# A tile's additions directly behind its last projection, token forms one place on, and weight rounds moved away from two places

## The chip, the cores and the metric

The kernel runs on one NeuronCore of one Trainium2 chip. Time is device microseconds (us) of that core for one execution; a version is compared by the median of its runs. The engines are TensorE (PE; PEld is its weight load), VectorE (DVE), ScalarE (ACT), GpSimd (POOL) and SyncE (SP, which issues most DMA transfers). Each engine runs its own instructions in program order and waits for the others by semaphores.

## The reference

Linear attention with decay over 2 x 8 sequences of 768 tokens (head size 64, blocks of 64 tokens), then two feed-forward layers over the 1536 tokens of width 512, all in float32:

```
out[block] = ((q @ k.T) * decay) @ v + (q * lam_pow) @ kv_state      # attention, block by block
kv_state   = lam_block * kv_state + (k * rev_pow).T @ v
h = x @ w_in                                                         # layer 1: 512 -> 2048
x = where(h >= 1, h, where(h <= -1, 0, (h + 1)**2 / 4)) @ w_out      #          2048 -> 512
gate = sigmoid(x @ w_gate); val = x @ w_val                          # layer 2: 512 -> 1536
out  = (gate * val) @ w_out                                          #          1536 -> 512
```

## The kernel before

**Numbers.** Weights arrive as pairs of 32-bit words of a wider float. Each float32 operand of a matmul is split into a high part (`...h`, rounded by a ScalarE copy) and the rest (`...l`, a VectorE subtraction), and a product is three matmuls: high by high, rest by high, high by rest (L211 to L213, L265, L397). A matmul of 128x128 by 128x512 is the unit of work.

**Weight pieces.** The weights are 68 pieces of 128x512. A *weight round* (`w_round`, `w_steps`) works on three pieces at once: it copies the words of piece k from the loaded `raw` tile (ScalarE, L102 and L103: tiles `wr` and `wc`), makes the float of piece k-1 (VectorE, L109, L110, L112) and splits piece k-2 into its high part (ScalarE, L116) and its rest (VectorE, L120) in a tile `w`. It also issues the next load (SP, L95). For some pieces GpSimd forms sums of weights (L135), which are split into the tiles `s` (ScalarE L142, GpSimd L143). In the attention, `w_round_in_two` does a round in two halves, with its additions on GpSimd.

**Attention.** Sixteen units (tile numbers in `s`, `uu`, `x`). In the loop over units, iteration i puts on the queues the scores and state updates of unit i+1, the evacuation of unit i-1, the states `sc`, the first half of a weight round for the i in `ROUNDS` (5 is the first), then `blocks(i + 1)`, which copies the states into the matmul operand `st` (ScalarE, L739), then the second half and the outputs of unit i (L749 and L758). Outputs of unit i need the blocks of unit i.

**Layer 1.** 16 slices of the hidden width in five groups (4, 3, 3, 3, 3) by three token tiles t of 512. For each (slice, tile), in the order of `seq`, TensorE computes the hidden block `h` (12 matmuls), ScalarE and VectorE make the activation `r` (L241, L242, L246), and `parts` splits it into `gh` and `gl` (L233, L234). The projection of the block two places back follows `h` on TensorE (12 matmuls, L265, into four accumulators `a`). When a group's last slice of a token tile is projected, `flush` adds the four accumulators to `part[t]` (VectorE, L287; in the first group copies, two on ScalarE at L283 and two on VectorE at L285). The accumulators and the `h` blocks share the eight banks of PSUM in a ring, so a bank's next user waits until its last reader is done.

Before the change, `finish` only projects and notes the tile in `closing`; `close` does the `flush` later, after the next hidden block and the next `split` have been put on the queues. After each projection, `go_on` takes the next entry of the list `later`, if there is one, and then does a weight round unless the entry returned True:

```
def go_on():
    if not (later and later.pop(0)()):
        w_round()
```

`flush` fills `later` at the last group: `x_split` splits the finished sums into the operands `xh` and `xl` of layer 2 (L297, L298), and `x_forms` (after t = 1) adds four entries for the *token forms*: sums and differences of token tiles 0 and 1 (`sub`, L375) and their splits (L379, L380) into `xt`.

**Layer 2.** 12 slices in pairs. The first pair is computed directly (`single`): hidden blocks of the gate and the value, sigmoid (L466), product (L467), projection. The other pairs use block products (`pair`, L397): seven blocks of 6 matmuls over token tiles 0 and 1, made from token forms and weight forms, which replace eight; ScalarE copies intermediate sums out of the first bank `p0` at L417, L423 and L428, and TensorE goes on adding to the same bank. Token tile 2 is computed by `single`. Layer 2 opens two new pools of four banks each, on the memory of the old eight.

Of the kernel before, what the change touches and what calls it, by code (L numbers as in the profile page):

```python
# [30 lines left out]
ROUNDS = (5, 6, 8, 10, 11, 12, 13, 14, 15)  # L31
# [8 lines left out]
def fused_kernel(ctx: ExitStack, tc: tile.TileContext, qkv, qd, cst, w1, w2, out):  # L40
# [232 lines left out]
    later = []  # L273

    def flush(n, t, js=range(4)):
        two = n >= NF1
        begin = n == (NF1 + GF if two else GROUPS[0]) - 1
        end = n == (NF1 + NF2 if two else NF1) - 1
        for j in js:
            o = part[t][:, j]  # L280
            if begin:
                if j % 2 == 0:
                    act.activation(o, accs[j], AF.Copy)  # L283
                else:
                    dve.tensor_copy(out=o, in_=accs[j])  # L285
            else:
                dve.tensor_tensor(out=o, in0=o, in1=accs[j], op=ALU.add)  # L287
            if end and two:
                r0 = t * TT + j * P
                sp.dma_start(out=out[r0:r0 + P, :], in_=o)  # L290
        if end and not two:
            tt = slice(t * TT, (t + 1) * TT)

            def x_split(js):
                for j in js:
                    o = part[t][:, j]
                    act.activation(xh[:, j, tt], o, AF.Copy)  # L297
                    dve.tensor_tensor(out=xl[:, j, tt], in0=o, in1=xh[:, j, tt].bitcast(F32),  # L298
                                      op=ALU.subtract)


            if t < NTT - 1:
                later.extend([lambda: x_split((0, 1)), lambda: x_split((2, 3))])
            else:
                later[2:2] = [lambda: x_split(range(4))]
            if t == 1:
                x_forms()

    behind, fresh, closing = [], [], []

    def close():
        if closing:
            flush(*closing.pop())

    def go_on():

# [7 lines left out]

    def feed_forward():
        def finish():  # L330
            p = behind.pop(0)
            project(*p, now=False)
            if p[4]:
                closing.append(p[:2])
            go_on()

        for u in seq:
            n, t, first, last = u
            h = hidden(n, t, 0)
            split()  # L340
            close()
            yield
            r = act1(h, n, t)
            act1_end(r, h)
            fresh.append((u, r))
            yield
            while attention_over and len(behind) >= 2:
                finish()
        split()
        while behind:  # L350
            close()
            finish()
        close()

# [9 lines left out]
    def x_forms():  # L366
# [7 lines left out]
        def sub(o, a, b_):  # L374
            dve.tensor_tensor(out=o, in0=a, in1=b_, op=ALU.subtract)  # L375

        def split(i):
            hi, lo = dst[i]
            act.activation(hi, f[i], AF.Copy)  # L379
            dve.tensor_tensor(out=lo, in0=f[i], in1=hi.bitcast(F32), op=ALU.subtract)  # L380
# [1 line left out]


        later.extend([
            lambda: sub(x1, y1, x1) or sub(y1, y2, y1),
            lambda: sub(y2, y2, x1) or sub(x2, x2, y2) or True,
            lambda: split(0) or split(2) or True,
            lambda: split(1) or split(3),
        ])

    def product(o, w, c, x, start):
# [136 lines left out]
    with ExitStack() as actx:  # L528
# [248 lines left out]
        with tc.manual_schedule():  # L777
# [13 lines left out]
            for i in range(nu):  # L791
# [13 lines left out]
                else:  # L805
                    split()
                r = w_round_in_two() if i in ROUNDS else iter((0, 0))
                next(r)
                if i + 1 < nu:
                    blocks(i + 1)  # L810
                next(r)
                if i in HIDDEN:
                    next(steps)
                outputs(i)
# [88 lines left out]
```

## Time and profile before

| | |
|---|---|
| runs before | 616.96, 619.74 and 618.11 us; median 618.11 us |
| profiled execution | 618.94 us, with a span of 616.1 us from first to last instruction |
| TensorE busy | 597.6 us (97%) |
| VectorE busy | 431.5 us (70%) |
| ScalarE busy | 323.5 us (53%) |
| GpSimd busy | 111.2 us (18%) |
| mean granted TensorE clock | 0.992 |
| chain that ended last | TensorE 88%, VectorE 4%, DMA 4%, ScalarE 2% |

The table is read from the top: one engine is busy nearly all the time, so the question for any change is where that engine stands still. A busy share is a mean over the whole span; the views by stretch and by wait tell where the idle time lies. A granted clock of 1.00 is the upper level (2.4 GHz), 0.50 the lower (1.2 GHz). In the timeline a row of several instructions shows their common time, and the times of one engine's rows overlap a little.

### The profile page before, as it was taken

The numbers are of one execution on the slowest core, as the hardware profiler recorded it, in microseconds if no ns is written. First come the engines' busy times: TensorE is split into PE (matmuls) and PEld (weight loads), VectorE is DVE, ScalarE is ACT, GpSimd is POOL, SyncE is SP. The second block draws the span as 40 slices with busy tenths as digits, with TensorE's granted clock in tenths as the row PEclk, the third lists the DMA queues.
The fourth block names the chain that finished last, engine by engine and source line by source line (L and its number), as shares of the span: only waits on it lengthen the run. The fifth ranks groups of instructions, "written<-read, shape, count | busy, mean of one in ns | idle before, by whom it ended". The sixth has DMA issues, their size and how long they took to land.

```text
span 616.1 us, 7965 instructions
## 1 busy us (share of the span) xinstructions
PE 597.6 (97%) x3016; PEld 488.2 (79%) x3016; DVE 431.5 (70%) x701; ACT 323.5 (53%) x585; POOL 111.2 (18%) x116
## 2 busy tenths in 40 slices
PE   7999999999999999999958999999999999999997
PEld 4787888888888888888847887888888888878886
DVE  7688853777576577477693789698598598595444
ACT  6798654675565465466462467554454454441220
POOL 4379500000000000000000132341151051050000
PEclk9999999999999999999987999999999999999999
DMA  9993410223132023033020123223023033000013
GB/s 293 399 321 129 145 61 2 89 89 96 35 103 69 23 80 104 0 103 102 2 79 23 35 68 104 66 72 103 16 86 103 8 96 104 0 1 0 1 69 136
DMA packets 15813, 52.58 MB, mean 85 GB/s; under 512 B 1688, under 2 KB 2976, under 8 KB 15776
## 3 DMA queue, kind: packets, MB, share of 16 engines
q1 hardware_dynamic: 15760, 52.08, 26.3%
q8 instruction: 23, 0.38, 0.2%
q14 instruction: 14, 0.11, 0.1%
q10 hardware_dynamic: 16, 0.01, 0.0%
HBM read 48.92 MB, written 3.15 MB: 85 GB/s over the span
## 4 chain that ended last, share of the span: by engine, by line
PE 88%; DVE 4%; DMA 4%; ACT 2%; issue 1%; DVEq 0%; ACTq 0%; SPq 0%
PE a L265 35%; PE p L397 15%; PE h L211 12%; PE h L212 11%; PE h L213 11%; DMA raw<-in_w 2%; PE x L758 1%; PE s L676 1%; PE x L749 1%; DMA qp<-pd 1%; DVE part L287 1%; DMA pd<-pw 1%; DVE wr L110 1%; DVE w L120 1%; PE uu L691 1%
## 5 line engine op out<-in xcount | busy, mean ns | idle before, releaser
L211 PE MATMUL h<-xh,w 128*128 128x512 f32 x320 | 126.3, 395 | 8.3 <-DVE part L287 8.3
L212 PE MATMUL h<-xh,w 128*128 128x512 f32 x320 | 125.6, 393 | 0.0
L213 PE MATMUL h<-xl,w 128*128 128x512 f32 x320 | 125.4, 392 | 0.0
L265 PE MATMUL a<-gh,w 128*128 128x512 f32 x384 | 118.6, 390 | 0.0
L265 PE MATMUL a<-w,gh 128*128 128x512 f32 x288 | 89.0, 390 | 0.1
L265 PEld LDWEIGHTS a<-gh,w 128*128 128x128 f32 x384 | 72.1, 188 | 15.1 <-POOL w L120 0.2
L246 DVE SCALAR_TENSOR_TENSOR r<-r,h 128x512 f32<-128x512 f32 x48 | 32.9, 686 | 70.7 <-ACT r L242 70.7
L241 ACT ACTIVATE r<-h,half 128x512 f32<-128x512 f32 x48 | 33.1, 689 | 88.3 <-PE h L213 88.3
L211 PEld LDWEIGHTS h<-xh,w 128*128 128x128 f32 x320 | 60.7, 190 | 21.7 <-DVE part L287 8.7
L135 POOL TENSOR_TENSOR wr<-wr 128x256 f32<-128x256 f32 x20 | 16.1, 806 | 339.8 <-DVE w L120 339.0
L287 DVE TENSOR_TENSOR part<-part,a 128x512 f32<-128x512 f32 x108 | 68.2, 680 | 12.3 <-PE a L265 12.3
L265 PE MATMUL a<-gl,w 128*128 128x512 f32 x192 | 74.9, 390 | 0.5 <-DVE gl L234 0.5
L212 PEld LDWEIGHTS h<-xh,w 128*128 128x128 f32 x320 | 60.7, 190 | 12.6
L213 PEld LDWEIGHTS h<-xl,w 128*128 128x128 f32 x320 | 60.6, 189 | 12.6
L265 PEld LDWEIGHTS a<-w,gh 128*128 128x128 f32 x288 | 54.1, 188 | 12.0 <-DVE part L287 0.6
L265 PE MATMUL a<-w,gl 128*128 128x512 f32 x144 | 56.7, 394 | 0.0
L234 DVE TENSOR_TENSOR gl<-r,gh 128x512 fp32r<-128x512 f32 x64 | 46.0, 719 | 11.9 <-ACT gh L233 11.9
L120 DVE TENSOR_TENSOR w<-wr,w 128x512 fp32r<-128x512 f32 x61 | 51.6, 846 | 1.8 <-ACT w L116 1.8
L116 ACT ACTIVATE w<-wr 128x512 fp32r<-128x512 f32 x68 | 42.3, 622 | 19.1 <-DVE wr L112 16.1
L233 ACT ACTIVATE gh<-r 128x512 fp32r<-128x512 f32 x64 | 40.0, 625 | 22.4 <-DVE r L246 13.0
L110 DVE SCALAR_TENSOR_TENSOR wr<-raw,wr 128x512 uint32<-128x512 uint32 x68 | 50.1, 737 | 2.3
L102 ACT ACTIVATE wr<-raw 128x512 f32<-128x512 f32 x68 | 45.0, 662 | 4.5 <-DMA raw<-in_w 2.1
(92 smaller groups left out, 876.3 us busy)
## 6 DMA issues: line engine op xcount, KB each, us to landing
raw<-in_w SPq DMA_DIRECT2D x68, 512.0 KB, 3.5
u<-in_qkv SPq DMA_DIRECT2D x12, 768.0 KB, 8.1
u<-in_qkv SPq DMA_DIRECT2D x8, 384.0 KB, 6.6
out<-part SPq DMA_DIRECT2D x12, 256.0 KB, 2.0
DT<-pd SPq DMA_DIRECT2D x1, 256.0 KB, 6.2
qp<-pd SPq DMA_DIRECT2D x2, 96.0 KB, 5.5
DT<-pd SPq DMA_DIRECT2D x1, 128.0 KB
cs<-in_cst SPq DMA_DIRECT2D x1, 98.0 KB, 2.0
```

What stands on the lines that cost most here:

```text
L102: act.activation(r, hi.bitcast(F32), AF.Copy, scale=2.0 ** -112)
L110: dve.scalar_tensor_tensor(out=ru, in0=hi, scalar=0x80000000, in1=ru, op0=ALU.bitwise_and, op1=ALU.bitwise_or)
L116: act.activation(ws[i][:, 0], tmps[i][1], AF.Copy)
L120: eng.tensor_tensor(out=ws[i][:, 1], in0=r, in1=ws[i][:, 0].bitcast(F32), op=ALU.subtract)
L211: pe.matmul(h, lhsT=wh, rhs=xh[:, k, tt], start=(k == 0), stop=False)
L212: pe.matmul(h, lhsT=wl, rhs=xh[:, k, tt], start=False, stop=False)
L213: pe.matmul(h, lhsT=wh, rhs=xl[:, k, tt], start=False, stop=(k == NP - 1))
L233: act.activation(gh, g, AF.Copy)
L234: dve.tensor_tensor(out=gl, in0=g, in1=gh.bitcast(F32), op=ALU.subtract)
L265: pe.matmul(accs[j], lhsT=a, rhs=b_, start=(first and m == 0), stop=(last and m == 2))
L287: dve.tensor_tensor(out=o, in0=o, in1=accs[j], op=ALU.add)
L397: pe.matmul(o, lhsT=a, rhs=b_, start=(start and k == 0 and m == 0), stop=(k == HK - 1 and m == 2), skip_group_check=True)
```

## The change

It changes only the order in which VectorE and ScalarE get their instructions; the lists of TensorE, GpSimd and SyncE and the number of instructions are as before. Four things move. `finish` projects and flushes in one step, so a tile's additions stand directly behind the `r` of the block before (and ahead of the weight round and the split that followed). The entries of `later` start one place later (`lambda: None` does nothing, and so a round follows). The first two subtractions of the token forms return True, so no round stands beside them, the first two splits get one, and two entries at the end give the place ahead of the block products no round. In attention unit 5, `blocks(6)` comes ahead of the first half of the weight round.

```
             if t < NTT - 1:
-                later.extend([lambda: x_split((0, 1)), lambda: x_split((2, 3))])
+                later.extend([lambda: None, lambda: x_split((0, 1)), lambda: x_split((2, 3))])
             else:
-                later[2:2] = [lambda: x_split(range(4))]
+                later[3:3] = [lambda: x_split(range(4))]
...
-    behind, fresh, closing = [], [], []
-
-    def close():
-        if closing:
-            flush(*closing.pop())
+    behind, fresh = [], []
...
         def finish():
-            p = behind.pop(0)
-            project(*p, now=False)
-            if p[4]:
-                closing.append(p[:2])
+            project(*behind.pop(0))
             go_on()
...
             split()
-            close()
             yield
...
         later.extend([
-            lambda: sub(x1, y1, x1) or sub(y1, y2, y1),
+            lambda: sub(x1, y1, x1) or sub(y1, y2, y1) or True,
             lambda: sub(y2, y2, x1) or sub(x2, x2, y2) or True,
-            lambda: split(0) or split(2) or True,
+            lambda: split(0) or split(2),
             lambda: split(1) or split(3),
+            lambda: None, lambda: True,
         ])
...
                 r = w_round_in_two() if i in ROUNDS else iter((0, 0))
-                next(r)
+
+                if i != ROUNDS[0]:
+                    next(r)
                 if i + 1 < nu:
                     blocks(i + 1)
-                next(r)
+                for _ in r:
+                    pass
```

What it does to three places follows; line numbers are those of each version, and the number behind a tile's name is its allocation. First VectorE at the step from layer 1 to layer 2, before: the end of a weight round (L120), the first two subtractions of the token forms (`part_79` is `part[0]`, `part_1004` is `part[1]`), a round, the additions of token tile 2 (`part_1005`), and the first product of layer 2.

```order
L120 TENSOR_TENSOR w_2993<-wr_2791,w_2993 128x512
L375 TENSOR_TENSOR part_79<-part_1004,part_79 128x1024
L375 TENSOR_TENSOR part_1004<-part_1004 128x1024
L109 TENSOR_SCALAR wr_2995<-wr_2995 128x512
L110 SCALAR_TENSOR_TENSOR wr_2995<-raw_2796,wr_2995 128x512
L112 ISA wr_2995<-wr_2995,wc_2996 128x1024
L120 TENSOR_TENSOR w_3019<-wr_2963,w_3019 128x512
L287 TENSOR_TENSOR part_1005<-part_1005,a_2_0_2938 128x512
L287 TENSOR_TENSOR part_1005<-part_1005,a_2_1_2942 128x512
L287 TENSOR_TENSOR part_1005<-part_1005,a_2_2_2946 128x512
L287 TENSOR_TENSOR part_1005<-part_1005,a_2_3_2950 128x512
L467 TENSOR_TENSOR r_0_3065<-r_0_3065,h_0_512_3052 128x512
```

The same place in the changed kernel.

```order
L120 TENSOR_TENSOR w_2993<-wr_2795,w_2993 128x512
L287 TENSOR_TENSOR part_1005<-part_1005,a_2_0_2938 128x512
L287 TENSOR_TENSOR part_1005<-part_1005,a_2_1_2942 128x512
L287 TENSOR_TENSOR part_1005<-part_1005,a_2_2_2946 128x512
L287 TENSOR_TENSOR part_1005<-part_1005,a_2_3_2950 128x512
L364 TENSOR_TENSOR part_79<-part_1004,part_79 128x1024
L364 TENSOR_TENSOR part_1004<-part_1004 128x1024
L457 TENSOR_TENSOR r_0_3053<-r_0_3053,h_0_512_3040 128x512
```

The four additions moved up to stand directly behind L120, the two subtractions (now L364) behind them, and the round away, behind later token forms.

Second ScalarE ahead of the first pair of block products, before: the last copy of `part[1]`, a weight round with two form copies (L142), the last `gh` of layer 2's first pair, the copy out of the first bank (L417), a round, and the next two copies and a sigmoid.

```order
L283 ACTIVATE part_1004<-a_1_2_3292 128x512
L116 ACTIVATE w_3368<-wr_3238 128x512
L102 ACTIVATE wr_3370<-raw_3243 128x512
L103 ACTIVATE wc_3371<-raw_3243 128x512
L142 ACTIVATE s_0_3377<-wr_3169 128x512
L142 ACTIVATE s_1_3380<-wr_3021 128x512
L233 ACTIVATE gh_2_3383<-r_2_3342 128x512
L417 ACTIVATE q_0_3390<-p_0_3387 128x512
L116 ACTIVATE w_3403<-wr_3305 128x512
L102 ACTIVATE wr_3405<-raw_3314 128x512
L103 ACTIVATE wc_3406<-raw_3314 128x512
L423 ACTIVATE q_1_3391<-p_0_3387 128x512
```

In the changed kernel (L407 and L413 are the copies of L417 and L423):

```order
L283 ACTIVATE part_1004<-a_1_2_3292 128x512
L233 ACTIVATE gh_2_3365<-r_2_3342 128x512
L407 ACTIVATE q_0_3372<-p_0_3369 128x512
L116 ACTIVATE w_3385<-wr_3238 128x512
L102 ACTIVATE wr_3387<-raw_3243 128x512
L103 ACTIVATE wc_3388<-raw_3243 128x512
L142 ACTIVATE s_0_3394<-wr_3169 128x512
L142 ACTIVATE s_1_3397<-wr_3100 128x512
L413 ACTIVATE q_1_3373<-p_0_3369 128x512
```

The round with the form copies moved from ahead of `gh` and the first copy to behind them, and so ahead of the second copy.

Third ScalarE in attention units 5 and 6, before: the scaled keys `kd`, the two word copies of the first weight piece, the blocks of unit 6, the evacuation `xh` of unit 5.

```order
L652 ACTIVATE kd_427<-u_177,DT 128x3x64 x2
L102 ACTIVATE wr_437<-raw_181 128x512
L103 ACTIVATE wc_438<-raw_181 128x512
L739 ACTIVATE st_99<-sc_97 64x3x64 x2
L769 ACTIVATE xh<-x_443 128x384
```

And in the changed kernel.

```order
L642 ACTIVATE kd_427<-u_177,DT 128x3x64 x2
L729 ACTIVATE st_99<-sc_97 64x3x64 x2
L102 ACTIVATE wr_439<-raw_181 128x512
L103 ACTIVATE wc_440<-raw_181 128x512
L759 ACTIVATE xh<-x_443 128x384
```

The blocks moved ahead of the two word copies.

## Rows read from the trace of the kernel before

**Rows 1.** The page: the span, and TensorE's busy time, share and instructions.

```profile
span 616.1 us, 7965 instructions
...
PE 597.6 (97%) x3016; PEld 488.2 (79%) x3016; DVE 431.5 (70%) x701; ACT 323.5 (53%) x585; POOL 111.2 (18%) x116
```

**Rows 2.** Waits of TensorE: us in total, times, longest.

```profile
PE h L211 <- DVE part L287: 8.3, 1, 8.3
PE x L758 <- ACT st L739: 1.5, 2, 1.1
...
PE p L397 <- ACT q L417: 1.0, 1, 1.0
```

**Rows 3.** Busy us (instructions) by stretch: PE, PEld, DVE, ACT, POOL; granted clock; DMA.

```profile
20.00:30.00 10.00, 8.94 (x124) 7.54 (x125) 6.75 (x19) 7.42 (x19) 3.00 (x3) 1.00 1.02 417
370.00:400.00 30.00, 29.03 (x127) 23.48 (x126) 23.91 (x36) 19.87 (x36) 8.15 (x8) 1.00 0.29 81
400.00:450.00 50.00, 50.00 (x220) 40.83 (x219) 39.74 (x59) 23.30 (x42) 14.22 (x13) 1.00 0.23 68
```

**Rows 4.** Timeline of TensorE around the layer step: start, us, instruction, [idle before].

```profile
316.56 0.39 PE L265 MATMUL a<-gl,w 128*128 128x512 f32 x1
325.26 0.80 PE L211 MATMUL h<-xh,w 128*128 128x512 f32 x1 [8.31 <-DVE part L287]
...
330.01 0.39 PE L213 MATMUL h<-xl,w 128*128 128x512 f32 x1
```

**Rows 5.** Timeline of VectorE at the same place.

```profile
317.25 0.68 DVE L120 TENSOR_TENSOR w<-wr,w 128x512 fp32r<-128x512 f32 x1
317.85 1.22 DVE L375 TENSOR_TENSOR part<-part,part 128x1024 f32<-128x1024 f32 x1
...
322.74 2.47 DVE L287 TENSOR_TENSOR part<-part,a 128x512 f32<-128x512 f32 x4
```

**Rows 6.** Half microseconds of that stop; granted clock behind the POOL column.

```profile
319.00:319.50 0.50, 0.00 (x0) 0.00 (x0) 0.47 (x2) 0.48 (x2) 0.00 (x0) 1.00 0.82 336
319.50:320.00 0.50, 0.00 (x0) 0.00 (x0) 0.50 (x1) 0.50 (x1) 0.00 (x0) 0.59 0.09 33
```

**Rows 7.** Chain that ended last, layer 1 and ahead of the first pair.

```profile
297.15 2.72 PE a L265 x12
...
371.09 0.62 ACT w L116
...
372.83 0.98 ACT s L142 x2
...
374.28 0.60 ACT q L417
```

**Rows 8.** Timeline of TensorE at the first pair of blocks.

```profile
371.08 0.62 PE L397 MATMUL p<-xh,w 128*128 128x512 f32 x2
...
374.92 0.73 PE L397 MATMUL p<-xth,s 128*128 128x512 f32 x2 [0.97 <-ACT q L417]
```

**Rows 9.** Timeline of ScalarE at attention units 5 and 6.

```profile
27.13 0.70 ACT L102 ACTIVATE wr<-raw 128x512 f32<-128x512 f32 x1 [2.08 <-DMA raw<-in_w]
...
28.29 0.72 ACT L739 ACTIVATE st<-sc 64x192 f32<-64x192 f32 x2
...
31.40 0.61 ACT L739 ACTIVATE st<-sc 64x128 f32<-64x128 f32 x2
```

**Rows 10.** Timeline of TensorE there: the state part of unit 6.

```profile
29.15 0.68 PE L758 MATMUL x<-qs,st 128*128 128x128 f32 x4 [1.06 <-ACT st L739]
```

**Rows 11.** Timeline of VectorE there: the states that the block copy reads.

```profile
25.31 0.59 DVE L717 SCALAR_TENSOR_TENSOR sc<-sc,qp,uu 128x64 f32<-128x64 f32 x2
```

**Rows 12.** Timeline of VectorE at a tile's end in layer 1.

```profile
287.69 0.69 DVE L246 SCALAR_TENSOR_TENSOR r<-r,h 128x512 f32<-128x512 f32 x1 [1.76 <-ACT r L242]
...
290.69 0.68 DVE L234 TENSOR_TENSOR gl<-r,gh 128x512 fp32r<-128x512 f32 x1
291.29 2.47 DVE L287 TENSOR_TENSOR part<-part,a 128x512 f32<-128x512 f32 x4
```

More of the change, by code (lines that the diff above doesn't have):

```diff
@@ L350, in feed_forward @@
         while behind:
-            close()
             finish()
-        close()
     HK = NP // 2
```

## The prediction

> **What bounds the kernel now.** I read the engine totals first, then who waits for whom, then the busy time by stretches, and the timeline only where those point. TensorE is busy 597.6 of 616.1 us [rows 1], so 18.5 us are all that any reordering can give back, and only where TensorE stands still. Its matmuls, weights and projections are not touched: the change moves additions, copies and weight rounds on VectorE and ScalarE alone, and TensorE issues the same list as before. So the question is which of TensorE's stops ends earlier. Three of its waits lie where the change moves something [rows 2]: one of 8.3 us for an addition at L287, 1.5 us for a copy at L739 (two waits, the longest 1.1 us) and one of 1.0 us for a copy at L417. By stretches, TensorE is idle 1.06 us between 20 and 30 us and 0.97 us between 370 and 400 us, and not at all between 400 and 450 us [rows 3]. Where it does not stop, a shorter queue on VectorE is worth nothing.
>
> The 8.3 us stop is the step between the layers. TensorE's last projection of layer 1 ends at 316.56 + 0.39 = 316.95 us and the next matmul starts at 325.26 us [rows 4]. It goes into the bank of the last accumulator of token tile 2, and that bank comes free when VectorE has added the accumulator to `part`. VectorE starts these four additions only at 322.74 us and ends them at 325.21 us, 0.05 us before TensorE goes on [rows 5]. Before them it runs two large subtractions (the token forms) and one weight round, from 317.85 us on.
>
> **Part 1: the additions ahead of the token forms, and no round at the sums.** In the new order the four additions follow VectorE's L120 directly, and the two subtractions come behind; the round that stood there moves behind the next sums. The last projection is over at 316.95 us, so the additions can start where the first subtraction started, at 317.85 us. With the 2.47 us that they took [rows 5] they end at 320.32 us, and TensorE goes on at 320.37 us in place of 325.26 us: **4.89 us** gained. Everything ahead of 317.85 us on VectorE keeps its order in this place, so I see no reason for a later start. What is late next: the two subtractions now lie behind the additions until 322.8 us, and the round behind the next token forms (a subtraction takes 1.22 us, so the round takes 4.89 less two of these, 2.45 us [rows 5]). Their cover is TensorE's own work. Twelve matmuls take 2.72 us at full clock [rows 7]; the first projection of layer 2 stands behind six such blocks, the first block that reads token tile 2 behind ten (eight blocks and two projections). That is 336.7 and 347.6 us at the earliest. VectorE has its last operand of that projection after the block that ends at 331.3 us and two operations of some 0.7 us, and can split token tile 2 (four operations, 2.5 us like the additions) right after the block that ends at 336.7 us, by about 341 us. So the two margins are some 4 and 6.6 us, more than a round. If that cover were gone, a round ahead of a needed operand would cost up to its 2.45 us.
>
> **Part 2: the clock behind the stop.** The granted clock is 1.00 until 319.5 us and 0.59 in the next half microsecond [rows 6]: about 2.6 us into the stop it fell from the upper level (2.4 GHz) to the lower (1.2 GHz), and it came back after TensorE had worked again. From 325.26 to 330.01 us TensorE started 11 matmuls [rows 4]; at full clock they take 11/12 of 2.72 us, 2.49 us [rows 7], so the low clock cost 4.75 - 2.49 = 2.26 us. The new stop lasts 320.37 - 316.95 = 3.42 us. That is more than the 2.6 us after which the clock fell here, and more than the 1.06 us stop at 29 us with which it stayed at 1.00 [rows 3]. The bounds are 0 (it falls again and stays low as long) and 2.26 us (it does not fall). Neither end has a row near it: I take **1.0 us**, on the view that it falls in more than half of the executions, and that the shorter stop then leaves a shorter slow stretch.
>
> The Trainium skill, page "TensorE: Matmul & The Clock Gate", section "HAM oscillation — how this bites in real kernels", says that an idle gap between bursts of matmuls sends the engine back to half rate, so that the next burst starts cold. The trace agrees for the stop of 8.3 us; for one of 3.4 us no row here shows it. By that rule this part would give nothing and the sum would be 6.5 us.
>
> **Part 3: no round ahead of the first pair of blocks.** TensorE's second block in the pair's first bank waits 0.97 us for ScalarE's copy at L417 [rows 8], which ran at 374.28 us [rows 7]. In the old order ScalarE did a weight round with two form copies and one more copy ahead of it. In the new order the round stands behind it, and only `gh` is left in front. The first bank's six matmuls start at 371.08 us and take half of 2.72 us, so they end at some 372.5 us; the copy then runs until 373.2 us, and TensorE is occupied by the second bank's block until 373.8 us. So the wait goes. What is late next is the copy at L423, which now stands behind that round: `w`, two word copies and two form copies, which took from 371.09 to 373.81 us in the old place, 2.7 us [rows 7]. It ends at about 373.2 + 2.7 + 0.6 = 376.5 us, and TensorE wants it after two more blocks, at 373.8 + 2.72 = 376.5 us. There is no margin, so I count **0.9 us** and not 0.97; the bounds are 0 (the new wait is as long as the old) and 0.97 us. The other rounds of layer 2 move by one place in the first two pairs and by none after that, in stretches where TensorE has no wait now [rows 3].
>
> **Part 4: attention unit 5.** ScalarE stands 2.08 us for the first weight load, copies its words at 27.13 us, and only then, at 28.29 us, writes the state blocks of unit 6 [rows 9]; TensorE waits 1.06 us for them, until 29.15 us [rows 10]. In the new order the block copy stands ahead of the words. Its last input is written by VectorE from 25.31 to 25.90 us [rows 11], so its 0.72 us fit wholly into the wait for the load, and TensorE loses nothing there: 1.06 us. A part is given back at once. ScalarE's run from the load on is shorter by the block copy alone, 0.72 us, and the blocks of unit 7, which TensorE needs next, end at 31.40 + 0.61 us today [rows 9]. So from there the gain is **0.72 us**. TensorE does not stop again until layer 1, and so it is carried on. Bounds: 0 (if the second load lands late) and 1.06 us.
>
> **Part 5: the other fourteen token tiles of layer 1.** Here the additions (for the first group of slices two copies on VectorE and two on ScalarE) go ahead of `gl`, and in some tiles ahead of a round too. For one such tile: VectorE ends L246 at 288.38 us, `gl` runs at 290.69 us, the additions at 291.29 us for 2.47 us [rows 12]. In the new order the additions run to 290.9 us, the round of 2.3 us to 293.2 us and `gl` to 293.9 us. The projection that reads this `gl` starts at 297.15 us [rows 7]. The margin is 3.2 us; the next L246 starts behind the same sum of work. So this costs nothing and, since TensorE has no wait there, gives nothing. If the cover were gone it would cost up to 2.47 us a tile.
>
> **Sum.** 4.89 + 1.0 + 0.9 + 0.72 = 7.5 us. The profiled execution took 618.94 us with a span of 616.1 us; it would take 611.4 us with a span of 608.6 us. The median of the runs, 618.11 us, is 0.8 us under the profiled time, so the forecast is 618.11 - 7.5 = **610.6 us**.
>
> **The rivals.**
> A. *Layer 2 takes it back.* TensorE arrives some 7 us earlier in work whose operands VectorE makes, and then waits for a round, a token form or the copy at L423. Against it: the margins of 4 and 6.6 us above, and no waits from 400 to 450 us. For it: VectorE is busy 23.9 of 30 us between 370 and 400 us [rows 3], and the copy at L423 has no margin. If parts 2 and 3 are lost and one round stands in the way, 4.89 + 0.72 - 2.45 = 3.2 us remain: 614.9 us.
> B. *The clock does not fall at all*: 1.26 us more than I count, 609.3 us. For it: the stop is less than half as long as the old one. Against it: 3.42 us is longer than the 2.6 us at which it fell.
> C. *The bank is not what holds TensorE.* If the first block of layer 2 needed something else that ends at about the same time, the stop would stay: gain 0.9 + 0.72, 616.5 us. Against it: the 0.05 us between the last addition and the first matmul.
> D. *Slower: `gl` is late in layer 1.* The place is the projection two blocks behind a tile's end; it decides once `gl` is more than 3.2 us later than now, where the sum above says 2.5 us. If each of fourteen tiles lost 1 us, the gain of 7.5 us would turn into a loss of 6.5 us: 624.6 us; from 0.54 us a tile there is no gain left.
>
> **How the numbers follow.** The forecast with the clock falling has 0.58, B 0.30, A 0.06, C 0.03, D 0.03. The likely cases lie between the sum of the lower bounds, 4.9 us (613.2 us), and that of the upper, 4.89 + 2.26 + 0.97 + 1.06 = 9.2 us (608.9 us). With half a microsecond for the runs, which lie up to 1.6 us from their median, the range is 608.4 to 613.7 us; A, C and D are left out. No change within 0.5% means 615.0 to 621.2 us, about what these runs can tell from nothing. Forecast, B and half of A are faster: 0.91; C and the rest of A the same: 0.06; D slower: 0.03.
>
> **What would show it.** Part 1: the wait of TensorE's L211 for L287 falls to about 3.4 us, with the four additions directly behind L120. Part 2: the granted clock of the 20 us from that stop on, and the spacing of the first 11 matmuls, 0.43 or 0.23 us. Part 3: no wait for L417, and at most 0.2 us for L423. Part 4: no TensorE wait at 28 us, and layer 1 starts 0.7 us earlier. Part 5: no new waits of projections for `gl`. The prediction is wrong if the stop stays over 5 us, or if TensorE's busy share falls behind 345 us.

## The result

The changed kernel takes 609.96 us, the median of 4 runs (608.39 to 612.54), beside 618.23 us (616.96 to 619.74) for the kernel before: the ratio is 0.9867, with a 95% interval of 0.9841 to 0.9893, 8.3 us faster. The profiled execution took 610.30 us with a span of 608.4 us. The forecast was 610.6 us.

The page of the changed kernel, as in [rows 1]: the span and TensorE's totals.

```profile
span 608.4 us, 7945 instructions
...
PE 596.9 (98%) x3016; PEld 487.4 (80%) x3016; DVE 429.4 (71%) x701; ACT 323.1 (53%) x585; POOL 110.9 (18%) x116
```

TensorE's work is the same (596.9 against 597.6 us of busy time) and its idle time fell from 18.5 to 11.5 us. The waits of TensorE in the changed kernel (us in total, times, longest), which answer to [rows 2]:

```profile
PE h L211 <- DVE part L287: 2.2, 1, 2.2
...
PE a L265 <- DVE gl L234: 0.5, 1, 0.5
PE a L265 <- DVE gl L433: 0.4, 1, 0.4
PE x L748 <- ACT st L729: 0.4, 1, 0.4
```

The wait for the additions went from 8.3 to 2.2 us, the waits for the state blocks from 1.5 to 0.4, and the one for ScalarE's copy out of the first bank (1.0) is gone. What is left of the waits for the state blocks lies at 11.56 us; the kernel before has the same one, 0.4 us at 11.73. One wait is new: 0.4 us for `gl` at L433. The wait for `gl` at L234 stands in the kernel before too, at 0.5 us.

By stretches, as in [rows 3] and [rows 6] (busy us and instructions of PE, PEld, DVE, ACT and POOL, granted clock, DMA):

```profile
20.00:30.00 10.00, 9.82 (x136) 8.24 (x134) 6.98 (x19) 7.67 (x20) 3.00 (x3) 1.00 1.02 417
318.00:318.50 0.50, 0.00 (x0) 0.00 (x0) 0.50 (x2) 0.00 (x0) 0.00 (x0) 1.00 0.93 360
318.50:319.00 0.50, 0.20 (x1) 0.20 (x2) 0.50 (x2) 0.00 (x0) 0.00 (x0) 0.56 0.86 352
321.50:322.00 0.50, 0.50 (x3) 0.37 (x2) 0.50 (x1) 0.00 (x0) 0.00 (x0) 0.53 0.00 0
322.00:322.50 0.50, 0.50 (x4) 0.41 (x3) 0.34 (x1) 0.00 (x0) 0.00 (x0) 1.00 0.00 0
370.00:400.00 30.00, 29.55 (x130) 23.86 (x129) 21.36 (x32) 16.59 (x30) 7.47 (x7) 1.00 0.22 71
```

The clock still falls in the stop between the layers, in the half microsecond from 318.5 on, and is back at 1.00 from 322.0 on. Between 370 and 400 us TensorE is busy 29.55 us in place of 29.03. The timeline of TensorE, for [rows 4], [rows 8] and [rows 10]:

```profile
28.19 0.71 PE L748 MATMUL x<-qs,st 128*128 128x128 f32 x4
...
31.09 1.29 PE L748 MATMUL x<-qs,st 128*128 128x128 f32 x6
...
316.18 0.39 PE L265 MATMUL a<-gl,w 128*128 128x512 f32 x1
318.80 0.79 PE L211 MATMUL h<-xh,w 128*128 128x512 f32 x1 [2.24 <-DVE part L287]
...
321.96 0.42 PE L212 MATMUL h<-xh,w 128*128 128x512 f32 x1
322.21 0.39 PE L213 MATMUL h<-xl,w 128*128 128x512 f32 x1
...
366.43 0.40 PE L387 MATMUL p<-xl,w 128*128 128x512 f32 x1
366.67 0.62 PE L387 MATMUL p<-xth,s 128*128 128x512 f32 x2
...
398.03 0.50 PE L265 MATMUL a<-w,gl 128*128 128x512 f32 x1 [0.45 <-DVE gl L433]
```

The last projection of layer 1 ends at 316.18 + 0.39 = 316.57 us and TensorE goes on at 318.80: a stop of 2.24 us, where 3.42 had been forecast. The matmuls from 318.80 to 321.96 stand some 0.43 us apart, those behind 322.21 some 0.23. At 366.67 the block that waited 0.97 us in [rows 8] follows at once. VectorE at the layer step, for [rows 5], and in the last two rows at the projection that waits for `gl`:

```profile
316.87 0.68 DVE L120 TENSOR_TENSOR w<-wr,w 128x512 fp32r<-128x512 f32 x1
317.47 2.48 DVE L287 TENSOR_TENSOR part<-part,a 128x512 f32<-128x512 f32 x4
319.86 1.22 DVE L364 TENSOR_TENSOR part<-part,part 128x1024 f32<-128x1024 f32 x1
321.12 1.22 DVE L364 TENSOR_TENSOR part<-part 128x1024 f32<-128x1024 f32 x1
...
394.83 0.67 DVE L425 TENSOR_TENSOR q<-q,p 128x512 f32<-128x512 f32 x1
396.14 1.84 DVE L433 TENSOR_TENSOR gl<-q,gh 128x512 fp32r<-128x512 f32 x1 [0.63 <-ACT gh L435]
```

The four additions stand directly behind L120, as the change says, and run from 317.47 to 319.95 us. But TensorE starts at 318.80, after two of them, and the chain that ended last says the same:

```profile
317.55 1.21 DVE part L287 x2
```

ScalarE, for [rows 9], at the first pair of blocks, and ahead of the late `gl`:

```profile
26.11 0.73 ACT L729 ACTIVATE st<-sc 64x192 f32<-64x192 f32 x2 [0.78 <-DVE sc L707]
27.56 0.69 ACT L102 ACTIVATE wr<-raw 128x512 f32<-128x512 f32 x1 [0.72 <-DMA raw<-in_w]
...
365.50 0.60 ACT L407 ACTIVATE q<-p 128x512 f32<-128x512 f32 x1 [0.92 <-PE p L387]
...
392.65 0.64 ACT L142 ACTIVATE s<-wr 128x512 fp32r<-128x512 f32 x1 [0.94 <-POOL wr L135]
394.95 0.64 ACT L142 ACTIVATE s<-wr 128x512 fp32r<-128x512 f32 x1 [1.66 <-POOL wr L135]
395.49 0.61 ACT L435 ACTIVATE gh<-q 128x512 fp32r<-128x512 f32 x1
```

### The profile page after: what moved, and what is told of

Read it like the earlier page. It is cut to its first block, busy times and chain, and to the rows that moved or that the text cites. A ratio compares the mean times of both kernels' runs of the same rounds, so it can differ in the third digit from the quotient of the medians.

```text
span 608.4 us, 7945 instructions
## 1 busy us (share of the span) xinstructions
PE 596.9 (98%) x3016; PEld 487.4 (80%) x3016; DVE 429.4 (71%) x701; ACT 323.1 (53%) x585; POOL 110.9 (18%) x116
## 4 chain that ended last, share of the span: by engine, by line
PE 87%; DVE 5%; DMA 4%; ACT 1%; issue 1%; POOL 1%; SPq 0%; DVEq 0%; ACTq 0%; POOLq 0%
PE a L265 35%; PE p L387 15%; PE h L211 11%; PE h L212 11%; PE h L213 11%; DMA u<-in_qkv 2%; DMA raw<-in_w 2%; PE x L748 1%; PE s L666 1%; PE x L739 1%; DVE wr L110 1%; DVE w L120 1%; DVE part L287 1%; DVE gl L433 1%; POOL wr L135 1%
## 5 line engine op out<-in xcount | busy, mean ns | idle before, releaser
L110 DVE SCALAR_TENSOR_TENSOR wr<-raw,wr 128x512 uint32<-128x512 uint32 x68 | 51.5, 758 | 2.3
L233 ACT ACTIVATE gh<-r 128x512 fp32r<-128x512 f32 x64 | 40.0, 625 | 20.9 <-DVE r L246 11.5
L120 DVE TENSOR_TENSOR w<-wr,w 128x512 fp32r<-128x512 f32 x61 | 48.9, 801 | 1.8 <-ACT w L116 1.8
L234 DVE TENSOR_TENSOR gl<-r,gh 128x512 fp32r<-128x512 f32 x64 | 44.6, 696 | 7.7 <-ACT gh L233 7.7
L112 DVE CUSTOM_DVE_ANT_0 wr<-wr,wc 128x1024 uint16<-128x1024 uint16 x60 | 45.2, 753 | 2.7
```

The costliest lines, as they stand in the source:

```text
L110: dve.scalar_tensor_tensor(out=ru, in0=hi, scalar=0x80000000, in1=ru, op0=ALU.bitwise_and, op1=ALU.bitwise_or)
L112: eng.tensor_tensor(out=ri, in0=ri, in1=c, op=ALU.add)
L120: eng.tensor_tensor(out=ws[i][:, 1], in0=r, in1=ws[i][:, 0].bitcast(F32), op=ALU.subtract)
L233: act.activation(gh, g, AF.Copy)
L234: dve.tensor_tensor(out=gl, in0=g, in1=gh.bitcast(F32), op=ALU.subtract)
```

## The experiments

Each ratio is to the kernel before in the same rounds: 618.70 us (617.11 to 620.51) for the first four runs below (step_only, other_tiles, sums_first, free_bank), 618.26 (617.33 to 620.51) for free_again and gh_first, 618.72 (617.06 to 619.61) for the others. To compare parts I use points of the traces: when TensorE's last projection of layer 1 ends, when its first matmul of layer 2 starts, and so on. A trace is of one execution.

**step_only: the layer step alone.** The kernel before, with only the last tile's additions moved directly behind its last projection.

```
-                later[2:2] = [lambda: x_split(range(4))]
+                later[3:3] = [lambda: x_split(range(4))]
...
-            if p[4]:
+            if p[:2] == (NF1 - 1, NTT - 1):
+                flush(*p[:2])
+            elif p[4]:
                 closing.append(p[:2])
```

> The kernel before with one edit: the four additions of the last token tile stand directly behind its last projection, ahead of the two subtractions and the round; all other tiles, the rounds and the attention as before. In this kernel the first block of layer 2 is given the bank of the fourth accumulator, as in the kernel before. Theory (the step between the layers holds most of the gain, and TensorE goes on after the addition that frees its bank): the stop falls from 8.3 to 3.4 us, that is by 4.9 us, and the low clock behind it costs 1 to 2.3 us as before; time 612 to 613.5 us. Rival one (TensorE always goes on after the second addition when they stand behind L120): the stop is 2.2 us. Rival two (the gain lies in the rounds left out or in the other tiles): 618 us.

It took 612.51 us (611.58 to 612.87), ratio 0.9902 (0.9882 to 0.9922). VectorE's additions in its timeline:

```profile
318.49 2.48 DVE L287 TENSOR_TENSOR part<-part,a 128x512 f32<-128x512 f32 x4
```

And TensorE around the stop:

```profile
317.21 0.39 PE L265 MATMUL a<-gl,w 128*128 128x512 f32 x1
321.02 0.50 PE L211 MATMUL h<-xh,w 128*128 128x512 f32 x1 [3.42 <-DVE part L287]
```

The additions end at 318.49 + 2.48 = 320.97 us and TensorE goes on 0.05 us later, after the fourth. The stop is 3.42 us, to the hundredth what part 1 of the prediction gives. So part 1 was right for this edit alone, and the other 1.2 us of the changed kernel come from another edit.

**other_tiles: all tiles but the last.** The kernel before, with the additions of all other tiles moved and those of the last left where they were.

```
-                later.extend([lambda: x_split((0, 1)), lambda: x_split((2, 3))])
+                later.extend([lambda: None, lambda: x_split((0, 1)), lambda: x_split((2, 3))])
...
-            if p[4]:
+            if p[4] and p[:2] != (NF1 - 1, NTT - 1):
+                flush(*p[:2])
+            elif p[4]:
                 closing.append(p[:2])
```

> The kernel before with the additions of all other token tiles of layer 1 directly behind their last projection, and the last tile's additions late as before. In this kernel the first block of layer 2 is given the bank of the second accumulator, since banks are given in the order in which they come free. Theory (moved additions cost nothing in layer 1, and which of the four additions frees the bank is set by the tiles before): no new waits of projections for gl, and the stop ends after the second addition, 7.1 us instead of 8.3; time 1.2 us less, 617.0 us. Rival (gl is late in layer 1): waits of L265 for L234 in 14 tiles, above 620 us. Rival (which addition frees the bank is set by the last tile's own order): stop 8.3 us, 618.2 us.

It took 617.26 us (616.57 to 617.90), ratio 0.9977 (0.9965 to 0.9990). VectorE's additions at the layer step:

```profile
323.08 2.47 DVE L287 TENSOR_TENSOR part<-part,a 128x512 f32<-128x512 f32 x4
```

TensorE there:

```profile
316.91 0.39 PE L265 MATMUL a<-gl,w 128*128 128x512 f32 x1
324.41 0.79 PE L211 MATMUL h<-xh,w 128*128 128x512 f32 x1 [7.12 <-DVE part L287]
```

The additions still come late, behind both subtractions and a round, but TensorE goes on at 324.41 us, after the second: 323.08 plus two of 0.62 is 324.3. The stop is 7.12 us in place of 8.31. In layer 1 nothing got slower: the one wait of its projections for `gl` at L234 is 0.5 us as before, and from the first hidden block to the end of the last projection it takes 277.58 us, beside 277.55 before and 277.57 in the changed kernel.

The allocation in the programs says why. The pool that opens with layer 2 hands out its banks in the order 4, 7, 6, 5, so the first hidden block gets bank 4 in all four kernels. Which accumulator of layer 1's last tile lies in bank 4 depends on the ring before it, in which nearly every tile gets the bank that came free first in the order of the program, and so on the place of every release:

| kernel | banks of the last tile's accumulators 1 to 4 | who held bank 4 | stop, us |
|---|---|---|---|
| before | 3, 2, 0, 4 | fourth | 8.31 |
| step_only | 3, 2, 0, 4 | fourth | 3.42 |
| other_tiles | 6, 4, 0, 2 | second | 7.12 |
| changed | 6, 4, 0, 2 | second | 2.24 |

Moving the other tiles' additions moved the accumulators of the last tile to other banks. An addition takes 0.6 us, so two of them are 1.2 us.

**sums_first: the two subtractions ahead of the additions.** The changed kernel, still without a round there, but with the old order of subtractions and additions at the last tile.

```
-            project(*behind.pop(0))
+            p = behind.pop(0)
+            end = p[:2] == (NF1 - 1, NTT - 1)
+            project(*p, now=not end)
             go_on()
+            if end:
+                flush(*p[:2])
```

> The changed kernel with the two subtractions of the token forms ahead of the last tile's additions again, still without a round beside them. Theory (each VectorE operation ahead of the additions is paid in full): the stop is 2.2 + 2.45 = 4.7 us against 2.2 us in the changed kernel, time 612.4 us or, with a longer slow stretch, up to 613.4 us. Rival (leaving out the round at the sums is what matters, the place of the additions is not): 610.0 us.

It took 613.76 us (613.11 to 614.21), ratio 0.9920 (0.9902 to 0.9937). VectorE at the layer step:

```profile
317.62 1.22 DVE L368 TENSOR_TENSOR part<-part,part 128x1024 f32<-128x1024 f32 x1
318.87 1.23 DVE L368 TENSOR_TENSOR part<-part 128x1024 f32<-128x1024 f32 x1
320.02 2.47 DVE L287 TENSOR_TENSOR part<-part,a 128x512 f32<-128x512 f32 x4
```

TensorE there:

```profile
321.35 0.80 PE L211 MATMUL h<-xh,w 128*128 128x512 f32 x1 [4.58 <-DVE part L287]
```

The stop is 4.58 us, 2.34 more than in the changed kernel: the two subtractions of 1.22 us. The time is a little above the 612.4 to 613.4 us expected: the slow stretch behind the stop is longer too, with 18.79 us for the first six blocks of layer 2 against 17.94 in the changed kernel. The round is the difference to other_tiles, which has the same bank and a round between the subtractions and the additions: 7.12 - 4.58 = 2.54 us (2.45 in part 1). So the old stop of 8.31 us is made up of 2.24 that remain, 2.34 for the subtractions, 2.54 for the round and 1.19 for the bank.

**free_bank and free_again: a bank with no reader.** The changed kernel, with one tile opened and let go ahead of layer 2, so that the first block gets bank 7, where no accumulator of the last tile lies. VectorE writes one element of that tile, and nothing reads it.

```
     def second_layer():
+        dve.memset(bank("skip")[:, 0:1], 0.0)
```

> The changed kernel with one more VectorE write of one element into a spare tile of the new pool, so that the first block of layer 2 is given a bank that came free long ago, and the second block the bank of the first accumulator. Theory (what is left of the stop, 2.2 us, is the wait for that bank alone, and the clock fell because of it, 1.6 us): no stop for L287, granted clock 1.00 throughout, 3.0 to 3.8 us less than the changed kernel, 606.5 us. Rival (the operands of layer 2, made by VectorE and ScalarE, are the next bound): a wait of similar length for gl or xl a few blocks later, 609 to 610 us.

> The changed kernel with a free bank for the second layer's first block, once more, as the partner of the run before in the same rounds and for the clock: no stop between the layers, the clock at 1.00 through the layer step, about 606.9 us, 0.45 us more than its partner if the queue on ScalarE sets the wait for gl. Rival: without a stop the clock can fall all the same, and single executions lie 1.5 to 2.3 us above.

They took 606.95 us (605.64 to 607.95), ratio 0.9809 (0.9788 to 0.9831), and 606.41 us (605.68 to 607.00), ratio 0.9809 (0.9796 to 0.9822): faster than the kernel before and the changed kernel. TensorE at the layer step of the first:

```profile
316.53 0.39 PE L265 MATMUL a<-gl,w 128*128 128x512 f32 x1
316.76 0.39 PE L211 MATMUL h<-xh,w 128*128 128x512 f32 x1
```

VectorE's additions there:

```profile
317.83 2.47 DVE L287 TENSOR_TENSOR part<-part,a 128x512 f32<-128x512 f32 x4
```

TensorE goes from the projection into layer 2 with no stop, over a microsecond before the first addition begins. So at this place only the bank held it; none of its operands did. From the first matmul of layer 2 to the first projection, which stands behind the sixth block, it takes 16.32 us here and 17.94 in the changed kernel, so the restart and the low clock had cost 1.62 us. With a restart at full clock, in step_only, the six blocks take 16.47 us; so 0.15 of it is the restart. The clock is 1.00 through this stretch in the profiled executions of free_bank, free_again and step_only.

**blocks_first: the attention edit alone.** The kernel before, with only this:

```
-                next(r)
+                if i != ROUNDS[0]:
+                    next(r)
                 if i + 1 < nu:
                     blocks(i + 1)
-                next(r)
+                for _ in r:
+                    pass
```

> The kernel before with only the attention units' edit: the five block copies of the state stand ahead of the weight words on ScalarE. Theory: TensorE's wait for the state (1.06 us at 29.15) goes to nothing or to the 0.4 us that the changed kernel keeps in the next unit, the rest of the kernel stays: 0.57 to 0.72 us faster than before, ratio about 0.999, the waits for the additions (8.3) and for ScalarE's sum (0.97) unchanged. Rival: the weights' words, now later, make a weight late in the first layer and the gain is lost: no faster than before, and a wait for w or wr in TensorE's list that was not there.

It took 618.08 us (616.88 to 619.09), ratio 0.9990 (0.9980 to 1.0000), which alone would not tell it from nothing. The trace does: the waits for L739 have left the list of TensorE's waits, and from the state updates of unit 6 to the first hidden block TensorE takes 39.95 - 25.19 = 14.76 us, against 39.40 - 24.09 = 15.31 before and 39.00 - 24.26 = 14.74 in the changed kernel. That is 0.55 to 0.57 us less. But the same stretch takes 14.63 us in other_tiles, which has no edit in the attention, so its length alone does not show what the edit is worth. What else moves it is the landing of the first weight load. Times from the start of unit 6's state updates:

| kernel | edit in the attention | ScalarE's first word copy, us | TensorE's state part of unit 9, us | difference |
|---|---|---|---|---|
| before | no | 3.04 | 13.19 | 10.15 |
| other_tiles | no | 2.11 | 12.26 | 10.15 |
| changed | yes | 3.30 | 12.63 | 9.33 |
| free_again | yes | 3.02 | 12.28 | 9.26 |

In all twelve traces the difference is 10.15 to 10.17 us without the edit and 9.26 to 9.35 with it. So at an equal landing of the load the edit is worth 0.8 to 0.9 us.

**round_kept: the round ahead of the block products put back.** The changed kernel without the last line of the list of entries.

```
-            lambda: None, lambda: True,
```

> The changed kernel with the weight round ahead of the block products of the first pair put back where it was. Theory: the wait of TensorE for ScalarE's sum (0.97 us before the change) returns, the new wait for VectorE's low part gl on ScalarE's side of the pair (0.45 us in the changed kernel) goes, so that the whole is 0.5 us slower than the changed kernel, about 610.5 us beside 610.0 in the same rounds. Rival 1: the new wait does not come from the round left out: both waits stand, 0.97 us slower, about 611. Rival 2: neither wait sets anything, since later waits take the time up: the same to 0.1 us. The stop between the layers stays at 2.2 us in all three.

It took 609.71 us (609.65 to 611.80), beside 609.41 us (608.40 to 611.07) for the changed kernel in the same rounds: the medians don't separate them; 0.5 us had been expected. TensorE's wait for ScalarE in the list of waits:

```profile
PE p L386 <- ACT q L406: 1.0, 1, 1.0
```

TensorE's timeline at the pair of blocks and at the projection with `gl`:

```profile
368.65 0.72 PE L386 MATMUL p<-xth,s 128*128 128x512 f32 x2 [0.98 <-ACT q L406]
...
399.08 0.61 PE L265 MATMUL a<-w,gh 128*128 128x512 f32 x2
399.60 0.50 PE L265 MATMUL a<-w,gl 128*128 128x512 f32 x1
```

The wait of 0.98 us is back and the one for `gl` is gone: at 399.60 its matmul follows 0.52 us behind the row before, which holds two. From the pair's first matmul to the third block TensorE takes 3.86 us (3.84 before, 2.73 in the changed kernel); the projection with `gl` takes 2.92 us (2.93 before, 3.46 in the changed kernel); the pair's third and fourth blocks take 2.87 us (2.86 before, 2.75 in the changed kernel). Against the kernel before, leaving the round out gains 1.11 + 0.11 and costs 0.53: **0.69 us** net. The other traces bear it out: from the pair's first matmul to TensorE's last, the six with the round take 240.86 to 240.99 us, and the five without it and without gh_first's edit 240.18 to 240.33.

**gh_first: why `gl` is late.** On top of free_bank, ScalarE's `gh` of the second pair's first block ahead of the two copies `s` that wait for GpSimd.

```
-            w_round()
+            split = [n for n in forms if n not in ready]
+            w_steps()
             rb, gb = next(b), {}
-            ha = single(n0, 2, pair_act(n1, rb, gb))
+            xb = pair_act(n1, rb, gb)
+            next(xb)
+            for n in split:
+                w_forms_split(n)
+            ha = single(n0, 2, xb)
```

> The kernel with a free bank for the second layer's first block, and in each pair of the second layer ScalarE's rounding gh of the second pair's first block put ahead of the two copies s that wait for GpSimd's weight forms. Theory of the 0.45 us wait of TensorE for gl: it is the queue on ScalarE (the copies s wait 0.94 and 1.66 us for GpSimd, gh stands behind them), so with gh ahead of them gl comes about 0.5 us earlier, the wait goes, and the kernel takes 0.45 us less than its partner in the same rounds, with nothing slow later. Rival: gl is late by VectorE's own 1.84 us (0.69 elsewhere) beside GpSimd's work, and the wait stays at about 0.4 us wherever gh stands. Second rival: the copies s, now later, make TensorE wait for s in the next pair, and the time is the same or more.

ScalarE at that place:

```profile
392.33 0.63 ACT L435 ACTIVATE gh<-q 128x512 fp32r<-128x512 f32 x1 [3.22 <-DVE q L423]
392.87 1.14 ACT L142 ACTIVATE s<-wr 128x512 fp32r<-128x512 f32 x2
```

VectorE's `gl`:

```profile
393.00 0.69 DVE L433 TENSOR_TENSOR gl<-q,gh 128x512 fp32r<-128x512 f32 x1
```

TensorE's projection that reads it:

```profile
394.35 0.62 PE L265 MATMUL a<-w,gh 128*128 128x512 f32 x2
394.81 0.39 PE L265 MATMUL a<-w,gl 128*128 128x512 f32 x1
```

No wait for `gl` is left: the projection takes 2.72 us, against 3.48 in free_again. So the wait goes when `gh` no longer stands behind the copies `s`, which waited 0.94 and 1.66 us for GpSimd. That the queue on ScalarE alone set it is not shown, since the run moves a second thing: `gl` took 0.69 us here, ahead of GpSimd's L143 at 393.56, and 1.84 us beside it in the changed kernel. There `gl` started at 396.14 and TensorE wanted it at 398.03 - 0.45 = 397.58 us; with 0.69 us it would have ended at 396.83 and held nobody up, late start or not. By these numbers the late start and the slow operation made the wait together. It took 606.40 us (605.29 to 608.02), ratio 0.9804 (0.9791 to 0.9818), beside 606.41 for its partner: the gain of 0.7 us is seen in the trace and not in the medians. Its profiled execution lost 0.84 us ahead of layer 2, with the clock at 0.57 and 0.58 from 10 to 14 us, where it was 1.00 in free_again.

**after_again and step_again: the clock.** The changed kernel and step_only, unchanged.

> The changed kernel once more, for the clock. Theory: what TensorE did ahead of the stop between the layers and the 2.2 us of the stop are the same in each execution, so that the granted clock falls again late in it and the 7 or 8 matmuls behind it are slow: 610.0 us. Rival: where the stop falls against the clock's own beat decides, and it differs from execution to execution: no slow matmuls in this one, and up to 1.6 us less, about 608.4.

> The kernel with only the last tile's additions put straight behind its last projection, once more, for the clock. Theory that the same program meets the same clock: the stop of 3.4 us, and no slow matmul behind it, as in its first execution: 611.6 us. Rival, that the clock's beat stands otherwise in each execution: the clock falls within the stop, and some 8 to 11 matmuls behind it take 0.43 in place of 0.23 us, 1.6 to 2.3 us more, about 613.5.

The changed kernel's four runs took 610.39, 608.40, 608.42 and 611.07 us, with a mean clock of 0.997, 1.000, 1.000 and 0.994. step_again's six took 610.73, 614.97, 614.63, 614.23, 610.83 and 612.53 us at 1.000, 0.992, 0.997, 0.997, 1.000 and 0.997 (median 613.38, ratio 0.9911, 0.9887 to 0.9936). By these mean clocks the rival holds in both: the same program meets the clock otherwise from execution to execution. Only the first execution of each has a trace, so where the clock fell in the others is not known; it need not be the stop, since in the profiled executions of other_tiles and gh_first it was low from 10 to 14 us as well (0.52 and 0.63, 0.57 and 0.58). Where at the stop it falls differs too. In round_kept the stop of 2.2 us ended at 319.52 us; by half microseconds:

```profile
319.50:320.00 0.50, 0.48 (x2) 0.43 (x3) 0.50 (x2) 0.00 (x0) 0.00 (x0) 1.00 0.69 279
...
320.50:321.00 0.50, 0.50 (x3) 0.36 (x3) 0.50 (x2) 0.00 (x0) 0.00 (x0) 0.56 0.00 0
```

The clock fell a microsecond after TensorE had gone on. In after_again the stop lay from 316.81 to 319.04 us:

```profile
318.50:319.00 0.50, 0.00 (x0) 0.00 (x0) 0.50 (x2) 0.00 (x0) 0.00 (x0) 0.79 0.96 393
```

Here it fell within the stop. In the profiled executions of step_only and step_again it stayed at 1.00 through a stop of 3.4 us.

## Why the prediction came out as it did

By the points of the traces, TensorE's last matmul of the trace starts 611.94 - 604.19 = 7.75 us earlier, which is made up of these (us gained):

| part | forecast | measured | where |
|---|---|---|---|
| 4, attention unit 5 | 0.72 | 0.57 | 15.31 to 14.74, as above; the start was 0.17 later |
| 1, the additions earlier | 4.89 | 4.89 | 8.31 to 3.42, step_only |
| 5, the other tiles | 0 | 1.19 | the rest of the stop, 3.42 to 2.23 by these points; alone 8.31 to 7.12 |
| 2, the clock | 1.0 | 0.68 | first six blocks of layer 2: 18.62 to 17.94, not fixed by the program |
| 3, the first pair of blocks | 0.9 | 0.69 | 1.11 + 0.11 - 0.53 |
| later start, and rest | 0 | -0.27 | -0.17; -0.02 in layer 1; -0.08 behind the second pair |
| sum | 7.5 | 7.75 | |

The median fell by 8.3 us and the profiled execution by 8.6: the time outside the span, 2.8 us in the profiled execution before, is 1.9 here.

**Part 1** was right in its mechanism and its size. **Part 5 is the step that failed**, together with the sentence in the first part that TensorE's first block goes into the bank of the last accumulator. That is so in the kernel before, and I carried it over to the changed kernel, where it is the second. I asked of the fourteen other tiles only whether their `gl` would come late (it does not), and found that they give nothing; they gave 1.19 us, since they moved the releases that decide which bank is handed out. That the sum came out close is luck: this gain, the shortfalls of the other parts (0.32, 0.21 and 0.15 us) and the lost 0.27 us nearly cancel.

**Part 2** had the right direction in the two executions compared: the clock fell again in the changed kernel's and the slow stretch was shorter, 8 matmuls in place of 11. With the restart it cost 1.62 us and not 1.26. The ground given, that the length of the stop decides, does not hold. The clock fell with a stop of 2.2 us and not with one of 3.42. And where it fell, the first six blocks of layer 2 took 18.62 us behind the stop of 8.31 us, 17.90 behind 7.12 (other_tiles), 18.79 behind 4.58 (sums_first), and 17.94 and 18.07 behind 2.2 (the changed kernel, round_kept): a shorter stop did not leave a shorter slow stretch. So the 0.68 us belong to these two executions. Rival B, the clock not falling, is what single executions show: 608.40 and 608.42 us at a mean clock of 1.000. In four of the changed kernel's eight executions the mean clock was 0.999 or 1.000: about half, where I had taken it to fall in more than half.

The rule of the Trainium skill, page "TensorE: Matmul & The Clock Gate", section "HAM oscillation — how this bites in real kernels", by which a burst behind an idle gap starts cold, agrees with the changed kernel's profiled execution (0.56 in the half microsecond in which TensorE restarts). But this part gave 0.68 us and not nothing; the profiled executions of step_only and step_again, at 1.00 behind 3.4 us, do not show it, and in round_kept the burst started at 1.00 and the clock fell within it.

**Part 3** removed its wait as said, and L413 makes TensorE wait nowhere. What was not seen is one pair later: the round now behind the first copy brings GpSimd's weight forms later, the `s` copies wait for them at the head of ScalarE's queue, `gh` and `gl` come late, and `gl` is slow beside GpSimd. This is rival A in small, 0.53 us and not 4.3.

**Part 4** gave 0.57 and not 0.72 us, and with the start 0.17 us later layer 1 began 0.40 us earlier, not 0.7. TensorE has no wait at 28.19 us, but it still waits for the next unit's blocks: its row at 31.09 us takes 1.29 us, where another row of six such matmuls takes 0.94 (at 36.89). The first load came at 27.56 in place of 27.13 us [rows 9] while TensorE ran only 0.17 later. By the table at blocks_first this later load took 0.26 us of an edit that is worth 0.8: the mechanism held, and its size in one execution hangs on the load.

Rivals C and D are out: free_bank shows that the bank alone held TensorE, and other_tiles that `gl` in layer 1 held TensorE no longer than before.

## What to carry to other kernels

When a wait is for a buffer that a pool hands out, look up in the changed program which buffer the waiting instruction gets, and who held it last: any edit that moves a release can change that, also one far away that costs nothing itself. Before work is reordered to free a buffer sooner, try giving the waiting instruction another one; here one opened tile was worth 3 us more. When work is moved out of a queue at one place, follow it: where it now stands, it can wait for a third engine and hold up what lies behind it. And before a stretch of one trace is put down to an edit, look at the same stretch in traces without the edit.

## What the runs showed of the hardware

Worked out from the half microseconds in which it fell, the granted clock fell 2.0 to 3.4 us from the start of the stop between the layers (2.0 in the changed kernel and in after_again, 2.2 in blocks_first, 2.6 before, 2.8 in sums_first, 3.2 in round_kept, 3.4 in other_tiles), and in round_kept TensorE had then been at work again for 1 us. Executions of one program that differ in their mean clock lie up to 4 us apart: in step_again 610.73 us at 1.000 and 614.97 at 0.992. What decides in which execution it falls was not tried and stays open.

A VectorE operation on 128x512 elements took longer while GpSimd worked beside it: `gl` at L433, 0.69 us elsewhere, took 1.84 us at 396.14 in the changed kernel, as GpSimd ran this from 394.88 on:

```profile
394.88 2.55 POOL L143 TENSOR_TENSOR s<-wr,s 128x512 fp32r<-128x512 f32 x2
```

In gh_first `gl` took 0.69 us, at 393.00. In the changed kernel an operation that reads one operand from the bank `p` kept its time beside GpSimd (L425, 0.67 us at 394.83). The Trainium skill, page "GPSIMD Engine Reference", section "1. Specifications", says that GpSimd shares its interfaces to SBUF with VectorE, and that VectorE's instructions with two inputs in SBUF contend for them; these three rows agree. Two inputs are not the whole condition: in the kernel before, L109, which reads one operand, took 0.42 us at 396.44 and 1.52 us at 399.94, beside GpSimd's L143 (397.97 to 401.18). So `gl` at L433 both started late and was slow.
